# Key sums in head pairs without a pack, and the second matrix of the first expert rounded later, by ScalarE

## The chip, the cores and the metric

The kernel runs on one core of a Trainium2 chip. The time is that of one launch in microseconds on the device; three launches of the kernel before took 662.1, 662.74 and 663.9, the median is 662.74.

## What is computed

A random-feature attention of 8 batches, 8 heads, 576 positions and 64 values a head feeds a layer of 8 experts, of which each token uses one. From the reference, cut:

```python
q_p, k_p = (phi(q_s), phi(k_s))                # exp(proj - max), 128 features
kv = np.einsum('bhsm,bhsd->bhmd', k_p, v)
z = np.sum(k_p, axis=2)
num = np.einsum('bhsm,bhmd->bhsd', q_p, kv)
den = np.einsum('bhsm,bhm->bhs', q_p, z)[..., None] + 1e-06
x = (num / den)                                # 4608 tokens of 512
logits = xn @ en.T / tau                       # 8 experts
h = np.maximum(x[mask] @ w1[e], 0.0)           # 512 -> 1024
out[mask] = gate_w[mask, None] * (h @ w2[e])   # 1024 -> 512
```

## The kernel before

**Two stages.** To about 220 us a loop `for i in range(43)` does the attention, 128 tokens a tile, 36 tiles; the query side runs 6 iterations behind the key side (`LAG`). Iteration 31, say, makes the key features of tile 31, the query features of tile 25 and the results of tile 24. After the loop the experts run, 38 steps of 128 tokens, until the end of the span.

**One iteration.** TensorE projects keys and queries (`proj`), VectorE takes row maxima (`nmk`, `nmq`, L331), ScalarE takes exponentials (`ftk`, `ftq`, L338). The query features are turned by TensorE (`qtr`, L400, into the bank pair `nub`) and copied out half by ScalarE, half by VectorE (`qp`, L405). `num` (L417) multiplies them with the key sums `kvs` into `nub`; `num_out` on VectorE divides (`rr`, then `xr` L432 and `lg` L435). TensorE's next `qtr` writes the same banks, so it waits for `lg`.

**Key sums.** Two sequences of a batch pair are open at a time (b = 0, 1), and eight times in the loop one is closed: ScalarE copies the sums `kva` of even and odd heads to `kvs` (L361, two copies); GpSimd packs the values without their sum column into `xgp` (L363); in the next iteration TensorE turns the pack (`kvtr`, L372), VectorE copies it out (L376), TensorE multiplies with the expert vectors (L384), and VectorE writes these logits of the keys into `kvs` (L390). A head takes 73 columns of `kvs`: 64 values, their sum, 8 logits. The turns stand in iterations 6, 10, 15, 19, 24, 28, 33 and 37.

**Routing.** Every three iterations a group of three tiles is routed (`routed(g)`), a generator that is taken on in steps over the following iterations: GpSimd adds logits (L449) to `raw`; VectorE picks the expert (`mx`, `raw` L460, `sel` L465); TensorE counts; VectorE makes `base` (L481); GpSimd makes positions from it (L484, L449, L494) and scatters the rows of `xr`, one tile each, to memory (`xs`, L496). `xr` has 6 buffers: `xr` of tile 24, which VectorE writes in iteration 31, is written over tile 18's, whose scatter must have landed. VectorE and GpSimd (L425) wait for that.

**First expert.** From iteration 28 the eight weight parts of the expert that most of the tokens chose so far are loaded on SP (`first_weights(n)`, tile `rf`, 512 KB each; even n is the first matrix w1, odd n the second, w2), and in the iteration behind rounded to `h` (w1 by ScalarE L535, w2 by VectorE L537), with the remainder `l` by GpSimd in four pieces (L540). A matrix has two `rf` buffers. From iteration 37 on the generator `first_steps` fills TensorE with two steps of that expert; its w2 is multiplied only behind the loop. TensorE then needs a third tile of rows (`fs_x`), which SP loads when the last scatter has landed.

**Order.** The queues of all engines are filled in the order in which the code is called. Lists by iteration hold work that is put off: `mid`, `after`, `then`, `ends` run at four places of an iteration, and within a list in the order of the appends.

Of the kernel before, what the change touches and what calls it, by code (L numbers as in the profile page):

```python
# [55 lines left out]
def attention_moe(ctx: ExitStack, tc: tile.TileContext, qT, kT, v1, omT, emb, tau, w1q, w2q, xs, out):  # L56
# [222 lines left out]
    with ExitStack() as c1:  # L279
# [77 lines left out]

        def kv_closed(sb, b):
# [63 lines left out]
        def num_out(i):
# [6 lines left out]
            nc.vector.tensor_scalar(rr, pn[:, :, :, D], EPS, None, op0=ALU.add)  # L429
# [213 lines left out]
        later, fill = None, first_steps()  # L643
# [8 lines left out]
        for i in range(END + 1):  # L652
            iq = i - LAG
            st["now"] = i
            n = iq - 3 * GPICK - 7
            if 0 <= n < 2 * NQ:
                first_weights(n)
# [78 lines left out]
            if 0 <= n < 2 * NQ:  # L736
                at(ends, i + 1).append((first_split, n))
# [446 lines left out]
```

## Time and profile before

| | us |
|---|---|
| median of three launches | 662.74 |
| the profiled execution | 658.2 |
| its span, first to last instruction | 656.4 |
| TensorE busy | 631.7 (96%) |
| VectorE busy | 497.3 (76%) |
| ScalarE busy | 416.9 (64%) |
| GpSimd busy | 328.5 (50%) |

The granted clock of TensorE is 0.996 of its full level over the span. Busy time is a mean over two stages with different limits: within the loop ScalarE and VectorE are nearly always busy, behind it TensorE alone is. A row of the timeline gives the start, the duration, engine, line, operation, output<-input, count, and in brackets how long the engine sat idle before it and what released it.

### The profile page before, as it was taken

How to read it: one execution, taken by the hardware profiler on the slowest of the kernel's cores; microseconds unless marked ns; L12 is line 12 of the kernel's file. 1: busy time of each engine (PE TensorE's matmuls, PEld its weight loads, DVE VectorE, ACT ScalarE, POOL GpSimd, SP SyncE). 2: the span in 40 equal slices, each digit the busy share in tenths (PEclk: the TensorE clock that was granted, in tenths of full speed). 3: DMA queues.
4: the chain of work that ended last, by engine and by line, in shares of the span. 5: the costliest groups of instructions: out<-in, count | busy, mean ns of one | idle time of the engine just before them, and what ended most of it. 6: DMA issues, size and time to landing. Idle time of an engine off the chain costs nothing. (4 is left out here: it accounts for less than half of the span.)

```text
span 656.4 us, 18641 instructions
## 1 busy us (share of the span) xinstructions
PE 631.7 (96%) x6339; PEld 532.1 (81%) x6340; DVE 497.3 (76%) x952; ACT 416.9 (64%) x1074; POOL 328.5 (50%) x414
## 2 busy tenths in 40 slices
PE   8999999998889999999999999999999999999993
PEld 7899999988877787888788888888888888888872
DVE  4789888899888736778787777777768787777771
ACT  6899899899877236645656565656555656565430
POOL 2013443448885425474556364646455554646352
PEclk9999999999999999999999999999999999999998
DMA  7547667678832388588898888978697878887710
GB/s 252 177 148 228 196 202 212 214 243 285 261 125 97 118 308 259 156 237 198 237 211 223 208 227 190 240 193 232 178 244 184 236 192 196 225 208 212 187 64 34
DMA packets 142362, 131.89 MB, mean 201 GB/s; under 512 B 106742, under 2 KB 106870, under 8 KB 142272
## 3 DMA queue, kind: packets, MB, share of 16 engines
q1 hardware_dynamic: 135808, 110.04, 62.8%
q0 software_dynamic: 6320, 20.38, 7.9%
q8 instruction: 57, 0.93, 0.6%
q10 hardware_dynamic: 144, 0.26, 0.2%
q14 instruction: 33, 0.27, 0.1%
HBM read 83.78 MB, written 21.97 MB: 161 GB/s over the span
## 5 line engine op out<-in xcount | busy, mean ns | idle before, releaser
L241 PE MATMUL nu<-w2h,hl 128*128 (+1 forms) x288 | 113.9, 395 | 0.4 <-DVE hl L948 0.4
L241 PE MATMUL nu<-w2h,hh 128*128 (+1 forms) x288 | 113.9, 396 | 0.0
L241 PE MATMUL nu<-w2l,hh 128*128 (+1 forms) x288 | 113.8, 395 | 0.0
L241 PE MATMUL pa<-w1h,xl 128*128 (+1 forms) x280 | 110.8, 396 | 0.4 <-DVE xl L947 0.4
L241 PE MATMUL pa<-w1h,xh 128*128 (+1 forms) x280 | 111.1, 397 | 0.0
L241 PE MATMUL pa<-w1l,xh 128*128 (+1 forms) x280 | 110.6, 395 | 0.0
L909 ACT ACTIVATE pl<-pa 128x512 uint16<-128x512 uint16 x68 | 40.1, 594 | 94.2 <-PE pa L241 56.0
L905 DVE TENSOR_REDUCE wd<-t 128x1024 uint16<-128x1024 uint16 x68 | 90.0, 1325 | 1.7 <-DMA t<-pl 1.7
L338 ACT ACTIVATE ftk<-pjk,nmk 128x128 f32<-128x128 f32 x288 | 84.9, 427 | 6.3 <-DVE nmk L331 6.0
L207 POOL TENSOR_TENSOR w1l<-raww,w1h 128x1024 f32 x34 | 83.7, 2461 | 7.4 <-DVE w1h L206 5.5
L905 DVE TENSOR_REDUCE pl<-pa 128x512 uint16<-128x512 uint16 x68 | 46.6, 688 | 51.6 <-ACT pl L909 51.5
L338 ACT ACTIVATE ftq<-pjq,nmq 128x128 f32<-128x128 f32 x288 | 80.0, 430 | 8.7 <-DVE nmq L331 7.8
L207 POOL TENSOR_TENSOR w2l<-raww,w2h 128x1024 f32 x34 | 82.1, 2415 | 2.4 <-issue 2.4
L327 PE MATMUL pjq<-om,qt 64*128 64x128 f32 x576 | 75.6, 283 | 1.1 <-ACT ftk L338 0.7
L327 PE MATMUL pjk<-om,kt 64*128 64x128 f32 x576 | 76.3, 285 | 0.3 <-DVE om L602 0.3
L944 ACT ACTIVATE hh<-wd 128x1024 fp32r<-128x1024 f32 x34 | 36.1, 1062 | 60.2 <-DVE wd L905 54.3
L327 PEld LDWEIGHTS pjk<-om,kt 64*128 64x128 f32 x576 | 65.1, 190 | 2.9 <-DVE om L602 0.6
L271 POOL DMA_INDIRECT y<-xgp x20 | 22.7, 1136 | 87.6 <-DVE xgp L248 84.1
L241 PEld LDWEIGHTS nu<-w2h,hl 128*128 128x128 f32 x288 | 54.0, 188 | 13.9 <-DVE hl L948 0.8
L327 PEld LDWEIGHTS pjq<-om,qt 64*128 64x128 f32 x576 | 63.9, 188 | 1.6 <-ACT ftk L338 0.9
L241 PEld LDWEIGHTS nu<-w2l,hh 128*128 128x128 f32 x288 | 54.1, 188 | 13.1
L241 PEld LDWEIGHTS nu<-w2h,hh 128*128 128x128 f32 x288 | 54.1, 188 | 13.0
(311 smaller groups left out, 1270.0 us busy)
## 6 DMA issues: line engine op xcount, KB each, us to landing
raww<-w1q SPq DMA_DIRECT2D x38, 512.0 KB, 3.9
raww<-w2q SPq DMA_DIRECT2D x38, 512.0 KB, 5.2
qt<-qT SPq DMA_DIRECT2D x36, 256.0 KB, 4.3
kt<-kT SPq DMA_DIRECT2D x35, 256.0 KB, 3.0
xgp<-xs SPq DMA_DIRECT2D x20, 260.5 KB, 2.8
xg<-xs SPq DMA_DIRECT2D x18, 260.5 KB, 2.9
rf<-w1q SPq DMA_DIRECT2D x4, 512.0 KB, 5.6
rf<-w2q SPq DMA_DIRECT2D x4, 512.0 KB
```

Source lines behind the costliest of these rows:

```text
L207: il = nc.gpsimd.tensor_tensor(at(l, dp), raw, at(h, dp).bitcast(F32), op=ALU.subtract)
L241: done.append(nc.tensor.matmul(dst, x[:, c * P : (c + 1) * P], ws.rearrange("p o f -> p (o f)"), start=(begin and i == 0 and k == 0), stop ...
L271: w = nc.gpsimd.indirect_dma_start(out=out, out_offset=bass.IndirectOffsetOnAxis(ap=xg[:, PAY - 1 : PAY].bitcast(I32), axis=0), in_=xg[:, ...
L327: nc.tensor.matmul(st["pj" + w, i, a][:, c, :], st[w, i][r, c, :], om[r, :], start=True, stop=True)
L338: nc.scalar.activation(ft[:, h, :], pj[:, h, :], AF.Exp, bias=nm[:, h : h + 1])
L905: nc.vector.tensor_reduce(to, src.unsqueeze(2), axis=AX.X, op=ALU.max)
L909: nc.scalar.activation(planes[1][:, o : o + 512], halved(src)[:, :, 1], AF.Copy)
L944: nc.scalar.activation(hh, wd[:, 0:F], AF.Relu)
```

## The change

Even heads now keep their sum column ahead of the values, odd heads behind; `kvs` is laid out as four pairs of 146 columns: logits, sum, values of the even head, then values, sum, logits of the odd one. The 128 values of a pair touch, so TensorE turns them from `kvs` itself, and GpSimd's pack is gone. `num`, `num_out` and the logits' copy use views to match. All four roundings of w2 go from VectorE to ScalarE. Two tables say when a part is loaded (`WLOAD`, by iteration) and rounded (`WSPLIT`; 1 stands for the list `ends`, 0 for `mid`). Parts of w1 keep their iterations (ends of 29, 31, 33 and 35), those of w2 go from the ends of 30, 32, 34 and 36 to the middle of 37, 38, 40 and 41. The loads stand behind an iteration's other loads, where they stood ahead.

```diff
+WLOAD = {28: (0,), 30: (2, 1), 32: (4, 3), 34: (6,), 39: (5,), 40: (7,)}
+WSPLIT = {0: (1, 29), 2: (1, 31), 4: (1, 33), 6: (1, 35), 1: (0, 37), 3: (0, 38), 5: (0, 40), 7: (0, 41)}
...
         def kv_closed(sb, b):
-            kvs[sb, b] = p1.tile([P, H, D + 1 + E], F32, name=f"kvs{sb}_{b}", tag="kvs", bufs=2)
-            for a in range(2):
-                nc.scalar.activation(kvs[sb, b][:, 4 * a : 4 * a + 4, 0 : D + 1], kva[sb, b, a], AF.Copy)
-            kvc = xgp[NPRE][:, 0:DM].rearrange("p (h d) -> p h d", h=H)
-            nc.gpsimd.tensor_copy(
-                kvc.rearrange("p (c a) d -> p a c d", a=2), kvs[sb, b][:, :, 0:D].rearrange("p (a c) d -> p a c d", a=2)
-            )
+            kvs[sb, b] = p1.tile([P, 4, 2 * HW], F32, name=f"kvs{sb}_{b}", tag="kvs", bufs=2)
+            nc.scalar.activation(kvs[sb, b][:, :, E : HW], kva[sb, b, 0], AF.Copy)
+            nc.scalar.activation(kvs[sb, b][:, :, HW : HW + D + 1], kva[sb, b, 1], AF.Copy)
...
-                nc.tensor.transpose(tr[:, c * P : (c + 1) * P], kvc[:, 2 * c : 2 * c + 2, :].rearrange("p a d -> p (a d)"), ident)
+                nc.tensor.transpose(tr[:, c * P : (c + 1) * P], kvs[sb, b][:, c, E + 1 : E + 1 + P], ident)
...
         def first_split(n):
             q, (_, h, l) = n // 2, W[("w1", "w2")[n % 2]]
             raw = st["rf", n]
-            if n % 2 == 0:
-                nc.scalar.activation(h[:, 0, q, :], raw, AF.Copy)
-            else:
-                nc.vector.tensor_copy(h[:, 0, q, :], raw)
+            nc.scalar.activation(h[:, 0, q, :], raw, AF.Copy)
...
+        for n, (late, i) in WSPLIT.items():
+            at(ends if late else mid, i).append((first_split, n))
...
-            n = iq - 3 * GPICK - 7
-            if 0 <= n < 2 * NQ:
-                first_weights(n)
             if i < 2 or i >= 4:
                 load(i + (4 if i < 2 else 2))
             if i in (3, 4):
                 loadq(i - 3)
             loadq(iq + 2 if i > LAG - 1 else -1)
+            for n in WLOAD.get(i, ()):
+                first_weights(n)
...
-            if 0 <= n < 2 * NQ:
-                at(ends, i + 1).append((first_split, n))
```

The table `WSPLIT` is put into the lists before the loop; the old code appended a rounding at the end of an iteration, behind the routing steps that were listed already. So GpSimd's queue changes at the end of iteration 29 not only by the absence of the pack. Before (`xr_3047` is the row buffer of tile 18, `xr_3611` that of tile 22):

```order
L425 COPY xr_3611<-ids 128x1
L484 TENSOR_TENSOR base_3628<-base_3628,sel_127 128x24
L449 TENSOR_TENSOR base_3628<-base_3628 128x3x4
L449 TENSOR_TENSOR base_3628<-base_3628 128x3x2
L449 TENSOR_TENSOR pos_3632<-base_3628 128x3
L494 CAST posi_3636<-pos_3632 128x1
L496 DMA xs<-xr_3047,posi_3636 38016x576
L540 TENSOR_TENSOR w1l<-rf_3356,w1h 128x256 x4
L425 COPY xr_3744<-ids 128x1
```

And after, the same place on GpSimd (tile 18 is `xr_3042`, tile 22 `xr_3603`):

```order
L433 COPY xr_3603<-ids 128x1
L545 TENSOR_TENSOR w1l<-rf_3356,w1h 128x256 x4
L492 TENSOR_TENSOR base_3625<-base_3625,sel_127 128x24
L457 TENSOR_TENSOR base_3625<-base_3625 128x3x4
L457 TENSOR_TENSOR base_3625<-base_3625 128x3x2
L457 TENSOR_TENSOR pos_3629<-base_3625 128x3
L502 CAST posi_3633<-pos_3629 128x1
L504 DMA xs<-xr_3042,posi_3633 38016x576
L433 COPY xr_3738<-ids 128x1
```

The remainder of part 0, which waits for ScalarE's rounding, has moved ahead of the positions and the scatter of tile 18. Part 6 does the same at the end of iteration 35. On ScalarE in iteration 41 stood before, in a row (`ex` are the first steps' exponentials, `ftq` the query features):

```order
L553 ACTIVATE hp_4698<-fs_a_4826 128x512
L261 ACTIVATE ex_5169,totalp<-xgp_103,rt_p 128x8
L261 ACTIVATE ex_5171,totalp<-xgp_104,rt_p 128x8
L405 ACTIVATE qp_1_5029<-nub 128x512
L338 ACTIVATE ftq_0_5071<-pjq_0_5019,nmq_0_5036 128x128 x4
```

And after:

```order
L263 ACTIVATE ex_5161,totalp<-xgp_103,rt_p 128x8
L263 ACTIVATE ex_5163,totalp<-xgp_104,rt_p 128x8
L406 ACTIVATE qp_1_5016<-nub 128x512
L542 ACTIVATE w2h<-rf_4894 128x1024
L340 ACTIVATE ftq_0_5063<-pjq_0_5006,nmq_0_5028 128x128
```

A rounding has come between the copy of the turned queries and the features of the next ones; the same stands in iterations 37, 38 and 40. On GpSimd the remainders of w2 follow there. Before, between the scatters of tile 29 and tile 30 (`xr_4564` and `xr_4666`):

```order
L496 DMA xs<-xr_4564,posi_4982 38016x576
L462 COPY xr_4666<-raw_4899 128x8
L462 COPY xr_4770<-raw_4899 128x8
L462 COPY xr_4882<-raw_4899 128x8
L425 COPY xr_5064<-ids 128x1
L484 TENSOR_TENSOR base_5081<-base_5081,sel_127 128x24
```

And after (`xr_4538` and `xr_4639`):

```order
L504 DMA xs<-xr_4538,posi_4969 38016x576
L470 COPY xr_4639<-raw_4879 128x8
L470 COPY xr_4748<-raw_4879 128x8
L470 COPY xr_4862<-raw_4879 128x8
L545 TENSOR_TENSOR w2l<-rf_4894,w2h 128x256 x4
L433 COPY xr_5056<-ids 128x1
L492 TENSOR_TENSOR base_5073<-base_5073,sel_127 128x24
```

The remainder of part 7 stands there now. Those of parts 1, 3 and 5 stand between there and the scatters of iteration 36; before, that stretch held one, of part 7.

## Rows read from the trace of the kernel before

**Rows 1.** Windows: busy us (count) of PE, PEld, DVE, ACT, POOL; clock, DMA, GB/s.

```profile
160.00:170.00 10.00, 8.88 (x215) 8.27 (x214) 9.54 (x24) 9.74 (x34) 7.50 (x20) 1.00 0.87 280
200.00:210.00 10.00, 9.35 (x154) 7.79 (x150) 8.00 (x23) 6.88 (x26) 7.64 (x28) 1.00 0.22 82
220.00:230.00 10.00, 10.00 (x58) 8.19 (x58) 7.68 (x53) 2.72 (x5) 2.95 (x3) 1.00 0.40 138
```

**Rows 2.** Timelines of POOL, PEld and ACT around the turn of iteration 24.

```profile
115.89 0.62 POOL L363 COPY xgp<-kvs 128x512 f32<-128x512 f32 x1 [5.51 <-ACT kvs L361]
...
116.56 0.42 PEld L372 LDWEIGHTS kvtr<-ident,xgp 128*128 128x128 f32 x4 [0.27 <-POOL xgp L363]
...
122.35 0.60 ACT L405 ACTIVATE qp<-nub 128x512 f32<-128x512 f32 x1 [1.84 <-PE pjk L327]
```

**Rows 3.** Timeline of DVE in iterations 30 to 32.

```profile
154.25 0.69 DVE L331 TENSOR_REDUCE nmk<-pjk 128x4 f32<-128x512 f32 x1 [0.22 <-PE pjk L327]
...
157.82 0.69 DVE L432 TENSOR_TENSOR xr<-nub,rr 128x512 f32<-128x512 f32 x1
...
158.77 0.70 DVE L460 TENSOR_TENSOR raw<-raw,mx 128x24 f32<-128x24 f32 x1
...
161.09 0.68 DVE L405 COPY qp<-nub 128x512 f32<-128x512 f32 x1
```

**Rows 4.** Lines L537 and L465: count, ns min/median/max, first and last start.

```profile
L537 DVE CAST w2h<-rf x4: 686/788/1187, 152.8 to 188.3; 128x1024 fp32r<-128x1024 f32 x4
...
L465 DVE SCALAR_TENSOR_TENSOR sel<-raw,iotm x12: 173/183/645, 46.6 to 218.8; 128x24 bf16<-128x24 f32 x12
```

**Rows 5.** Timeline of PE, the turn of the queries in iteration 37.

```profile
188.52 0.71 PE L400 MATMUL nub<-ident,ftq 64*128 64x64 f32 x16 [0.60 <-DVE lg L435]
```

**Rows 6.** Timeline of ACT: roundings of w1, query features of iterations 40 and 41.

```profile
148.62 1.14 ACT L535 ACTIVATE w1h<-rf 128x1024 fp32r<-128x1024 f32 x1
...
184.06 1.14 ACT L535 ACTIVATE w1h<-rf 128x1024 fp32r<-128x1024 f32 x1
...
206.62 2.18 ACT L338 ACTIVATE ftq<-pjq,nmq 128x128 f32<-128x128 f32 x8 [1.13 <-DVE nmq L331]
...
211.22 2.18 ACT L338 ACTIVATE ftq<-pjq,nmq 128x128 f32<-128x128 f32 x8 [0.89 <-DVE nmq L331]
```

**Rows 7.** Timeline of POOL from iteration 29 to the last scatters.

```profile
150.23 1.05 POOL L496 DMA_INDIRECT xs<-xr,posi  x1 [0.86 <-POOL posi L494]
151.31 3.31 POOL L540 TENSOR_TENSOR w1l<-rf,w1h 128x256 fp32r<-128x256 f32 x4
...
183.48 0.23 POOL L484 TENSOR_TENSOR base<-base,sel 128x24 f32<-128x24 f32 x1
...
185.37 1.05 POOL L496 DMA_INDIRECT xs<-xr,posi  x1 [0.56 <-POOL posi L494]
...
193.00 2.78 POOL L540 TENSOR_TENSOR w2l<-rf,w2h 128x256 fp32r<-128x256 f32 x4
...
198.80 0.23 POOL L484 TENSOR_TENSOR base<-base,sel 128x24 f32<-128x24 f32 x1 [0.93 <-DVE base L481]
...
213.30 0.23 POOL L484 TENSOR_TENSOR base<-base,sel 128x24 f32<-128x24 f32 x1 [3.16 <-DVE base L481]
...
222.94 0.98 POOL L496 DMA_INDIRECT xs<-xr,posi  x1 [3.23 <-DVE runi L761]
```

**Rows 8.** Line L496 in 140:162, then in 190:222; and the page's DMA issues.

```profile
DMA to landing us min/median/max: 5.5/5.8/6.5
...
DMA to landing us min/median/max: 2.7/2.8/4.9
...
rf<-w1q SPq DMA_DIRECT2D x4, 512.0 KB, 5.6
```

**Rows 9.** Timelines of POOL and PE where the third tile of rows arrives.

```profile
231.57 0.60 POOL L765 DMA_DIRECT2D xs<-w1l  x1 [5.08 <-DMA xgp<-xs]
...
232.02 0.60 PE L227 MATMUL fs_x<-ident,xgp 128*128 128x128 f32 x4
```

More of the change, by code (lines that the diff above doesn't have):

```diff
@@ L356, in kvmm, with spread @@
                     )
+        HW = D + 1 + E
+        def spread(x, *dims):
+            return bass.AP(tensor=x.tensor, offset=x.offset, ap=[x.ap[0], *([a, n] for a, n in dims)])
         def kv_closed(sb, b):
-            kvs[sb, b] = p1.tile([P, H, D + 1 + E], F32, name=f"kvs{sb}_{b}", tag="kvs", bufs=2)
-            for a in range(2):
-                nc.scalar.activation(kvs[sb, b][:, 4 * a : 4 * a + 4, 0 : D + 1], kva[sb, b, a], AF.Copy)
-            kvc = xgp[NPRE][:, 0:DM].rearrange("p (h d) -> p h d", h=H)
-            nc.gpsimd.tensor_copy(
-                kvc.rearrange("p (c a) d -> p a c d", a=2), kvs[sb, b][:, :, 0:D].rearrange("p (a c) d -> p a c d", a=2)
-            )
-            st["kvc", sb, b] = kvc
+            kvs[sb, b] = p1.tile([P, 4, 2 * HW], F32, name=f"kvs{sb}_{b}", tag="kvs", bufs=2)
+            nc.scalar.activation(kvs[sb, b][:, :, E : HW], kva[sb, b, 0], AF.Copy)
+            nc.scalar.activation(kvs[sb, b][:, :, HW : HW + D + 1], kva[sb, b, 1], AF.Copy)
         def kv_turn(sb, b):
-            kvc = st["kvc", sb, b]
             st["kvtr", sb, b] = tr = ps.tile([P, 512], F32, name=f"kvtr{sb}_{b}", tag="kv0")
             for c in range(4):
-                nc.tensor.transpose(tr[:, c * P : (c + 1) * P], kvc[:, 2 * c : 2 * c + 2, :].rearrange("p a d -> p (a d)"), ident)
+                nc.tensor.transpose(tr[:, c * P : (c + 1) * P], kvs[sb, b][:, c, E + 1 : E + 1 + P], ident)
         def kv_turned(sb, b):
@@ L390, in kv_logits_out @@
             nc.vector.tensor_copy(
-                kvs[sb, b][:, :, D + 1 :].rearrange("p (a c) e -> p c a e", a=2),
+                spread(kvs[sb, b].rearrange("p c w -> p (c w)"), (2 * HW, 4), (HW + D + 1, 2), (1, E)),
                 st["kve", sb, b].rearrange("p c (a e) -> p c a e", a=2),
@@ L407, in qcopy, with heads @@
                 tc.declare_no_dep(c.ins, st["cp", 1].ins.name, reason="another bank")
-        pn = nub[:, :, 0 : 4 * (D + 1 + E)].rearrange("p a (h w) -> p a h w", h=4)
+        flat = nub.rearrange("p a x -> p (a x)")
+        o0 = P + E // 2
+        pn = [nub[:, a, o : o + 4 * HW].rearrange("p (h w) -> p h w", h=4) for a, o in ((0, o0), (1, 0))]
+        def heads(o, at1, n):
+            x = 512 + at1 - o0 - o
+            return flat[:, o0 + o : o0 + o + 2 * x].rearrange("p (a x) -> p a x", a=2)[:, :, 0 : 4 * HW].rearrange("p a (h w) -> p a h w", h=4)[:, :, :, 0:n]
         def num(i):
@@ L417, in num @@
                         nc.tensor.matmul(
-                            pn[z * 64 : z * 64 + 64, a, h, :], st["qp", i, z][:, 4 * a + h, :], kvs[sb, int(b)][:, 4 * a + h, :],
+                            pn[a][z * 64 : z * 64 + 64, h, :], st["qp", i, z][:, 4 * a + h, :], kvs[sb, int(b)][:, h, a * HW : (a + 1) * HW],
                             start=True, stop=True,
@@ L428, in num_out @@
             rr = small.tile([P, 2, 4], F32, name=f"rr{i}", tag="rr", bufs=3)
-            nc.vector.tensor_scalar(rr, pn[:, :, :, D], EPS, None, op0=ALU.add)
+            nc.vector.tensor_scalar(rr.unsqueeze(3), heads(E, D, 1), EPS, None, op0=ALU.add)
             nc.vector.reciprocal(rr, rr)
@@ L432, in num_out @@
             nc.vector.tensor_tensor(
-                xr[:, 0:DM].rearrange("p (h a d) -> p a h d", a=2, d=D), pn[:, :, :, 0:D], by(D), op=ALU.mult,
+                xr[:, 0:DM].rearrange("p (h a d) -> p a h d", a=2, d=D), heads(E + 1, 0, D), by(D), op=ALU.mult,
             )
             nc.vector.tensor_tensor(
-                st["lg", g][:, gi].rearrange("p (a h) e -> p a h e", a=2), pn[:, :, :, D + 1 :], by(E), op=ALU.mult,
+                st["lg", g][:, gi].rearrange("p (a h) e -> p a h e", a=2), heads(0, D + 1, E), by(E), op=ALU.mult,
             )
@@ L642, in attention_moe @@
             at(ends, i).append((f,))
-        later, fill = None, first_steps()
+        for n, (late, i) in WSPLIT.items():
+            at(ends if late else mid, i).append((first_split, n))
+        fill = first_steps()
         def go(d, *key):
@@ L1152, in layout @@
         rows = slice(0, D) if u == 4 else slice(D, P) if u == 5 else slice(0, P)
-        v1[:, u, rows, :, :D] = v[:, u - (u > 4), rows]
-        v1[:, u, rows, :, D] = 1
+        v1[:, u, rows, 0::2, 1:] = v[:, u - (u > 4), rows, 0::2]
+        v1[:, u, rows, 0::2, 0] = 1
+        v1[:, u, rows, 1::2, :D] = v[:, u - (u > 4), rows, 1::2]
+        v1[:, u, rows, 1::2, D] = 1
     v1 = v1.reshape(NSB * (TPS + 1), P, H, D + 1)
```

## The prediction

> **What bounds the kernel now.** I read the windows first. From 160 to 170 us VectorE and ScalarE are busy for 9.54 and 9.74 of 10 us and TensorE has gaps (8.88); from 200 to 210 TensorE is nearly full (9.35) while the others are not; behind 220 it has no gap at all [rows 1]. So a microsecond saved on VectorE or ScalarE counts up to iteration 36, when the key side ends, and from iteration 39 on the end moves only as TensorE's queue moves. TensorE's queue has one fixed appointment behind the loop: it turns the third tile of rows at 232.02, and those rows were in at 231.57, 0.45 us before [rows 9]. They are loaded when the last scatter has landed, so GpSimd's queue sets the other edge of the same instant. I therefore follow two clocks to 232: the loop's, and GpSimd's. Behind that the work is the same before and after.
>
> All sums are in the profiled execution: 658.2 us, of which the span is 656.4. Its 658.2 is 4.5 below the median of the launches, 662.74; I add the difference that I find to the median.
>
> **The pack.** GpSimd packs for 0.62 us, and TensorE's turn stood 0.27 us for it [rows 2]; the same wait stands at the other turns. Taking the copy away lets the turn start when the projections end, since the pack ended 0.27 us behind them; ScalarE's copies were done before the pack began. It counts only where TensorE is late: in iteration 24 ScalarE then sat 1.84 us for TensorE [rows 2], and iterations 6, 15 and 33 have the same pattern (double key sums). In the other four VectorE runs through and nothing is gained. That is 4 x 0.27 = 1.1 us: 0.8 before iteration 29 and 0.3 in iteration 33. The bounds are 0 (ScalarE's second copy takes the pack's place) and the whole pack, 4 x 0.62 = 2.5; I take the wait itself. The new strides of `kvs` and `nub` keep the counts and sizes of every copy and product, and the sums still come from the same banks; I cost them at nothing.
>
> **VectorE's four roundings.** They last 0.69 to 1.19, together about 3.4 us [rows 4]. What each was worth is what stood behind it. In iteration 30, VectorE waited 0.22 for TensorE right after it [rows 3]; the gain there is hidden anyway by the next item. In iteration 32 ScalarE has no gap [rows 1]; I take 0.1 of 0.69. In iteration 36 the next copy needs the turned queries, whose turn started at 188.52 on the release of `lg`, not of the rounding [rows 5]: 0. In iteration 34 VectorE is the bound and 0.6 of 0.69 counts (neighbouring rows overlap by 0.1). With them goes a second cost: `raw` took 0.70 in iteration 31 while GpSimd worked on remainders [rows 3, 7], and `sel`, whose median is 0.183, 0.645 [rows 4]. The same pair stands in iteration 34. Free of the remainders they are some 0.9 shorter together. In iteration 34 that goes, since the remainder of part 4 is then done early: 0.6 + 0.9 = 1.5 us. In iteration 31 it stays, because part 2's remainder moves right beside it.
>
> **What the order adds in iteration 29.** The remainder of part 0 now stands ahead of `base` on GpSimd. It waits for ScalarE's rounding, which ends at 148.62 + 1.14 = 149.76 [rows 6]; it takes 2.78 rather than the 3.31 that it took beside VectorE's rounding [rows 7]; from the start of `base` to the scatter pass 185.37 - 183.48 = 1.89 us [rows 7]. So tile 18's scatter starts at 149.8 + 2.8 + 1.9 = 154.5, where it was 150.23. Scatters of this stretch land 5.5 to 6.5 us after their start [rows 8]: at 160.0 to 161.0, say 160.5. VectorE writes `xr` of tile 24 over that buffer, which it did at 157.82 [rows 3]. Before, the landing came by 156.7; now VectorE stands, and behind it the logits, the next turn of the queries, their copies: iteration 32 starts 2.7 us later than before. [...]
>
> From there: +2.7, -0.1 (iteration 32), -0.3 (the turn in 33), -1.5 (34) = **+0.8 us in iteration 35**, still without the 0.8 saved before iteration 29.
>
> **ScalarE in the tail.** Its four new roundings (about 1.1 each, the form of L535) fall between the copy of the queries and the next features, where ScalarE waited 1.13 and 0.89 us for VectorE's maxima [rows 6]; two earlier gaps are as wide. I cost them at nothing. Uncovered they would cost 4.5 us. Behind them on ScalarE are only the features, and TensorE waits for those. Part 5 is loaded an iteration before its rounding, 206.62 - 211.22 apart, 4.6 us; such a load took 5.6 to land [rows 6, 8], so ScalarE may stand up to 1 us there. The DMA share is 0.22 then [rows 1]; I take 0.
>
> **GpSimd in the tail.** Between `base` at 183.48 and the last three scatters at 222.94 lie 39.5 us, of which GpSimd waited 0.93 + 3.16 + 3.23 = 7.3 [rows 7]; 32.1 us is work. The new queue begins this chain with part 6's remainder, which waits for ScalarE at 184.06 + 1.14 + 0.8 = 186.0 [rows 6]. Its work is 32.1 - 0.6 (pack) - 0.5 (part 6 beside no VectorE rounding) + 3 x 2.78 (parts 3, 5, 7; part 1 is in part 7's old place) [rows 7] = 39.3 us, and the waits are gone, because the chain is always behind. The last scatters start at 186.0 + 39.3 = 225.3, 2.4 later. The third tile is in at 231.57 + 2.4 = 234.0, and TensorE, due at 232.02 and late by less than that, turns it 1.9 later than before.
>
> **Sum.** +1.9 in the tail, -0.8 from the first three turns: **+1.1 us**. The profile would be 659.3, the launch 662.74 + 1.1 = 663.8 us.
>
> **Rivals.**
>
> *The scatter lands in time.* If it lands in 2.8 to 4 us as in the quiet stretch [rows 8], `xr` is not held beyond 157.8, and iteration 35 comes at -1.9 rather than +0.8: TensorE's appointment at -0.8, with the first turns -1.6: 661.1. If the pair in iteration 31 shrinks too, 1.4 more: 659.7. For it: part 1's load no longer stands in iteration 29. Against: all five scatters from 140 to 161 took 5.5 or more. GpSimd's queue caps this gain, the loop itself would have 3 us. Chance 0.25.
>
> *The burst of loads (slower).* Parts 2 and 1 are now issued back to back at the end of iteration 30's loads, about 153.5 to 155, by their place on SP just ahead of tile 18's scatter; before, 512 KB at most stood beside one. A second 512 KB at 250 to 300 GB/s [rows 1] is some 2 us more: landing after 8.5, iteration 32 at +5.2, the appointment at +4.4, in all +3.6: 666.3. It decides from a landing of 6.9 us: there the sum passes 0.3%. For it: the DMA share is already 0.87 [rows 1]. Chance 0.25. [...]
>
> *The pack is not saved, or part 5 comes late.* ScalarE's second copy holds TensorE as long as the pack did (+0.8), or ScalarE stands for part 5: 664.6. Chance 0.1.
>
> **How the numbers follow.** Forecast 0.40 with its own range of 662.3 to 665.3 (the landing 5.5 to 6.5, half a microsecond in GpSimd's chain), rivals 0.25, 0.25, 0.1. The predicted time is the forecast's, 663.8. The range reaches from the middle of the first rival to that of the second: 660.3 to 666.3. 0.3% is 2.0 us, about what a measurement of this kernel can tell from no change. Faster by more needs a time below 660.7: the lower part of the first rival, 0.16. Slower by more needs more than 664.7: nearly all of the burst and the upper end of the others, 0.30. Within: 0.54.
>
> **What would show it.** Right: in the profile after, VectorE's `xr` of iteration 31 or GpSimd's `ids` copy stands 2 to 3 us for the landing of tile 18's scatter, which starts near 154; iteration 34 is about 1.5 us shorter; GpSimd's waits of 3.16 and 3.23 near the loop's end are gone and the last three scatters start 1 to 2 us later; TensorE waits a little at `fs_x`. The turns wait for nothing on GpSimd. Wrong: `xr` in iteration 31 doesn't wait; ScalarE's w2 roundings push the query features; GpSimd is idle again before the last scatters, and then the loop's clock decides.

## The result, and the profile after

The changed kernel takes 670.66 us (median of five launches, 668.51 to 671.94), the kernel before 662.94 in the same comparison: a ratio of 1.0111 with a 95% interval of 1.0087 to 1.0135. Two later comparisons gave 1.008 [1.0051, 1.0109] and 1.0083 [1.0066, 1.010]. The change makes the kernel slower by 0.8 to 1.1%, some 5.4 to 7.7 us; 663.8 with a range of 660.3 to 666.3 was forecast.

One thing must be known before traces are compared. The chips fall into two kinds for this kernel. On some, the kernel before takes 657 to 658 us, on others 663 to 665 (each chip was met in one batch of runs only, so the chip and the occasion can't be told apart); its profiled execution of 658.2, on which the prediction rests, is like the launches of the first kind, and the changed kernel's first trace comes from the second. Both kernels are longer there in iterations 13 to 28, so this difference has no part in the result (shown below, by a trace of the kernel before from a chip of the second kind). Ratios below are always to the kernel before on the same chip, and the ledger of the time is made from two traces of one chip.

Windows of the changed kernel, with the columns of [rows 1]: the first row answers to 160 to 170 us there, and the others are finer.

```profile
160.00:170.00 10.00, 4.53 (x102) 4.27 (x100) 3.81 (x10) 4.66 (x15) 4.44 (x11) 0.85 0.71 236
...
160.00:162.00 2.00, 2.00 (x66) 1.93 (x62) 1.56 (x4) 2.00 (x10) 1.47 (x6) 1.00 0.93 164
162.00:164.00 2.00, 1.06 (x16) 0.86 (x16) 0.00 (x0) 1.40 (x6) 0.56 (x1) 1.00 0.94 358
164.00:166.00 2.00, 0.00 (x0) 0.00 (x0) 0.00 (x0) 0.94 (x1) 0.00 (x0) 1.00 1.03 403
166.00:168.00 2.00, 0.00 (x0) 0.00 (x0) 0.35 (x1) 0.00 (x0) 0.41 (x2) 0.75 0.62 241
168.00:170.00 2.00, 1.47 (x22) 1.47 (x24) 1.90 (x6) 0.31 (x1) 2.00 (x4) 0.50 0.04 17
170.00:172.00 2.00, 1.56 (x16) 1.30 (x16) 1.97 (x5) 1.10 (x5) 1.72 (x4) 0.50 0.00 0
172.00:174.00 2.00, 2.00 (x41) 2.00 (x42) 1.54 (x3) 1.89 (x9) 0.49 (x4) 0.54 0.42 117
174.00:176.00 2.00, 2.00 (x58) 1.93 (x54) 1.44 (x6) 2.00 (x9) 0.23 (x1) 1.00 0.40 156
```

In [rows 1] VectorE and ScalarE were busy for 9.54 and 9.74 of these 10 us. Now VectorE stands from 161.7 to 167.65, GpSimd from 162.6 to 167.6, TensorE from 163.1 to 168.5, and ScalarE from 164.9 to 169.7, while the DMA share is 0.93 to 1.03 up to 166. TensorE's granted clock is 0.51 from 167 to 168, 0.50 up to 172 and 0.54 in the two us behind. What they stand for is in the timelines. GpSimd (answers to [rows 7]), VectorE ([rows 3]), TensorE ([rows 5]) and SP's queue, iteration 31 of the changed kernel:

```profile
154.12 2.80 POOL L545 TENSOR_TENSOR w1l<-rf,w1h 128x256 fp32r<-128x256 f32 x4 [6.17 <-ACT w1h L542]
...
158.77 1.05 POOL L504 DMA_INDIRECT xs<-xr,posi  x1 [0.56 <-POOL posi L502]
...
167.59 0.18 POOL L433 COPY xr<-ids 128x1 int32<-128x1 int32 x1 [5.03 <-DMA xs<-xr,posi]
...
158.48 0.68 DVE L406 COPY qp<-nub 128x512 f32<-128x512 f32 x1
...
161.50 0.20 DVE L438 RECIPROCAL rr<-rr 128x8 f32<-128x8 f32 x1
167.65 0.69 DVE L440 TENSOR_TENSOR xr<-nub,rr 128x512 f32<-128x512 f32 x1 [5.95 <-DMA xs<-xr,posi]
...
171.08 0.67 DVE L406 COPY qp<-nub 128x512 f32<-128x512 f32 x1
...
168.53 1.12 PE L401 MATMUL nub<-ident,ftq 64*128 64x64 f32 x16 [5.47 <-DVE lg L443]
...
157.80 0.34 SPq L537 DMA_DIRECT2D rf<-w1q  x1
158.41 0.34 SPq L537 DMA_DIRECT2D rf<-w2q  x1
```

The remainder of part 0 (L545) ends just ahead of the routing step, tile 18's scatter starts at 158.77, 8.8 us later VectorE may write `xr`, and the iteration takes 12.60 us from copy to copy of the queries, where it took 6.15 (from 154.94 to the copy at 161.09 [rows 3]). Parts 2 and 1 of the weights were asked for one behind the other right ahead of the scatter.

### The profile page after: what moved, and what is told of

Its sections match the earlier page's. It is cut to its first block, busy times and chain, and to the rows that moved or that the text cites. A ratio compares the mean times of both kernels' runs of the same rounds, so it can differ in the third digit from the quotient of the medians.

```text
span 669.0 us, 18617 instructions
## 1 busy us (share of the span) xinstructions
PE 633.8 (95%) x6339; PEld 536.4 (80%) x6340; DVE 494.5 (74%) x948; ACT 421.4 (63%) x1078; POOL 321.3 (48%) x406
## 5 line engine op out<-in xcount | busy, mean ns | idle before, releaser
L329 PE MATMUL pjk<-om,kt 64*128 64x128 f32 x576 | 78.8, 294 | 0.8 <-DVE om L607 0.5
L329 PEld LDWEIGHTS pjk<-om,kt 64*128 64x128 f32 x576 | 67.0, 197 | 3.4 <-DVE om L607 0.8
```

The lines of the kernel that those rows point to most:

```text
L329: nc.tensor.matmul(st["pj" + w, i, a][:, c, :], st[w, i][r, c, :], om[r, :], start=True, stop=True)
```

## Where the time goes, on one chip

The length of an iteration is the time from its copy `qp` on VectorE to the next one. From the traces e13 (kernel before) and e14 (changed), both of one chip, whose launches differ by 5.6 us (665.12 and 670.74):

| stretch | forecast | e14 less e13 |
|---|---|---|
| iterations 7 to 28 | -0.8 | -1.7 |
| 29 and 30 | 0 | -0.4 |
| 31 | +2.7 | +6.4 |
| 32 to 36 | -1.9 | -0.2 |
| 37 to 41 | not the bound | +2.6 |
| sum to iteration 42 | | +6.7 |

The two spans differ by 6.8 us. By the loop's own clock the forecast's stretches add up to 0.0, the measured ones to 6.7: iteration 31 is 3.7 of the difference, iterations 37 to 41 are 2.6, iterations 32 to 36 1.7, and the early ones take 1.3 off. The forecast took GpSimd's chain for the later clock at `fs_x`, came to +1.9 there and so to +1.1 in all.

## The experiments

All verdicts are ratios to the kernel before in the same comparison. The lengths of the iterations that differ, in us (chips of the first kind above, of the second below):

| kernel | 31 | 32 | 34 | 37 | 38 | 40 | 41 |
|---|---|---|---|---|---|---|---|
| e10, before | 6.09 | 5.24 | 6.51 | 5.69 | 5.54 | 4.41 | 5.00 |
| e1, layout alone | 6.10 | 5.22 | 5.87 | 5.36 | 5.48 | 4.41 | 4.99 |
| e9, layout, ScalarE rounds in place | 6.33 | 5.41 | 5.28 | 5.66 | 5.50 | 4.41 | 4.99 |
| e2, weights alone | 11.99 | 5.87 | 5.19 | 6.98 | 5.67 | 7.72 | 6.47 |
| e3, w1 behind the routing | 5.45 | 7.11 | 5.24 | 5.36 | 5.53 | 7.15 | 6.34 |
| e4, loads spread | 9.18 | 6.96 | 5.27 | 7.13 | 5.48 | 7.30 | 5.24 |
| e11, parts 5 and 7 late | 6.52 | 5.12 | 5.17 | 5.36 | 5.49 | 6.34 | 6.24 |
| e12, the same, asked early | 6.53 | 5.11 | 5.17 | 5.36 | 5.48 | 4.69 | 5.24 |
| e13, before | 6.54 | 5.05 | 6.44 | 6.40 | 5.48 | 5.04 | 4.76 |
| e14, changed | 12.93 | 5.51 | 6.11 | 6.46 | 5.67 | 6.02 | 5.76 |
| e5, changed | 11.48 | 6.66 | 6.22 | 6.67 | 6.13 | 6.61 | 5.24 |
| e6, no late remainders | 5.79 | 7.03 | 5.22 | 6.01 | 8.46 | 6.43 | 5.14 |
| e7, w1 behind, loads spread | 5.69 | 6.32 | 5.22 | 6.00 | 8.47 | 5.86 | 5.24 |
| e8, w2 in 34 to 38 | 5.80 | 5.53 | 6.21 | 5.36 | 6.83 | 4.77 | 5.52 |
| e15, as e12 | 6.56 | 5.11 | 5.22 | 5.55 | 5.49 | 4.71 | 5.82 |

**The two halves.** e1 takes the change's `kvs`, `num` and `num_out` and leaves the weights as they were; e2 the reverse, with the pack. From the changed kernel to e1 (the roundings of w2 go back to VectorE besides):

```diff
-        for n, (late, i) in WSPLIT.items():
-            at(ends if late else mid, i).append((first_split, n))
...
-            for n in WLOAD.get(i, ()):
-                first_weights(n)
...
+            n = iq - 3 * GPICK - 7
+            if 0 <= n < 2 * NQ:
+                first_weights(n)
...
+            if 0 <= n < 2 * NQ:
+                at(ends, i + 1).append((first_split, n))
```

> Only the layout of the key sums is changed; loads, roundings and remainders of the first expert stand as before the change. Where the changed kernel went wrong, its trace shows three places: iterations 13 to 28 end 4.3 us later than in the trace before, iteration 31 takes 12.6 us instead of 6.2, and iterations 37 to 42 lose another 3.5. Theory W (all that counts comes from the weights, and the early 4.3 us are what one execution differs from another): the time is 662.1, that is 0.8 below the kernel before by my step on the pack, within 1 us of it either way; iterations 31 and 32 and 37 to 42 look as before. Theory L (the new layout itself makes the turns and the iterations behind them longer): 666 to 667, and iterations 13, 15, 19, 22, 24 and 28 show the lengths of the changed kernel (5.74, 7.55, 6.80, 6.44, 7.49, 6.50 us).

> Only the loads, roundings and remainders of the first expert are changed; the key sums keep the layout and the pack of before. Theory W: 670 to 672 (the changed kernel's time, or 0.8 above it), with the scatter that iteration 31 needs landing 8 to 9 us after its start. Theory L: 666 to 667, since the early 4 us stay away, and iteration 31 still takes 12 to 13 us.

The layout alone: 656.07 against 657.61, 0.9975 [0.9958, 0.9992], a gain of 1.5 us. The weights alone: 666.87, 1.0145 [1.010, 1.0189], a loss of 9.3. So the whole loss is the weights', and the layout is a small gain. Iterations 13, 15, 19, 22, 24 and 28 of e1 and e2 have the lengths of the kernel before within 0.2 us, but for iteration 13 of e2 (5.71 where e10 has 5.18).

**Order or loads.** e3 puts the first matrix's splits back behind the routing steps; e4 leaves the order and asks for parts 1 and 3 an iteration earlier.

In e3 the second piece stands at the end of the loop's body; the last two lines are e4.

```diff
-            at(ends if late else mid, i).append((first_split, n))
+            if not late:
+                at(mid, i).append((first_split, n))
...
+            for n, (late, j) in WSPLIT.items():
+                if late and j == i + 1:
+                    at(ends, j).append((first_split, n))
...
-WLOAD = {28: (0,), 30: (2, 1), 32: (4, 3), 34: (6,), 39: (5,), 40: (7,)}
+WLOAD = {28: (0,), 29: (1,), 30: (2,), 31: (3,), 32: (4,), 34: (6,), 39: (5,), 40: (7,)}
```

> The changed kernel, but the first matrix's splits (parts 0, 2, 4, 6) stand behind the routing steps of their iteration on GpSimd, as before the change; loads and everything else as changed. Theory O (the remainder ahead of the routing steps starts tile 18's scatter 4.3 us late, and that is most of it): the scatter starts about 4.3 us earlier against its iteration, lands in time or within 1.2 us of it even if it takes 8.8 us, iteration 31 takes 6.2 to 7.4 us instead of 12.6, and the time falls by 5 to 6.5 to 664 to 666. Theory B (the loads of parts 2 and 1 asked for together hold up whatever scatter runs beside them): iteration 31 or the next still waits 3 us or more, and the time falls by less than 3.

> The changed kernel, but parts 1 and 3 are asked for one iteration earlier than parts 2 and 4 (29, 30, 31, 32 instead of both at 30 and both at 32), so that no two 512 KB loads are asked for together; the order on GpSimd as changed. Theory B: tile 18's scatter lands some 6 us after its start instead of 8.8, iteration 31 takes 9 to 10 us, and the time falls by 2.5 to 4 to 667 to 668. Theory O: the scatter still starts late and what is gained is below 1.5; 669 to 671.

e3: 659.31, 1.003 [1.0003, 1.0057]. e4: 663.82, 1.0092 [1.0055, 1.0129]. Against the sum of the two halves, 665.4, an estimate for the changed kernel on this chip, e3 is 6.1 us faster and e4 1.6: the gain that theory O had for e3, and less than theory B had for e4. Iteration 31 takes 5.45 us with the old order and the burst, 9.18 with the new order and no burst, 11.99 with both (e2, which keeps the pack). GpSimd's scatter of tile 18 and VectorE's `xr` of tile 24 in e4, then the same two in e3, then in e2:

```profile
154.61 1.05 POOL L504 DMA_INDIRECT xs<-xr,posi  x1 [0.56 <-POOL posi L502]
...
160.00 0.69 DVE L440 TENSOR_TENSOR xr<-nub,rr 128x512 f32<-128x512 f32 x1 [2.53 <-DMA xs<-xr,posi]
```

```profile
149.55 1.05 POOL L504 DMA_INDIRECT xs<-xr,posi  x1 [0.56 <-POOL posi L502]
...
156.98 0.69 DVE L440 TENSOR_TENSOR xr<-nub,rr 128x512 f32<-128x512 f32 x1
```

```profile
154.95 1.05 POOL L498 DMA_INDIRECT xs<-xr,posi  x1 [0.56 <-POOL posi L496]
...
163.26 0.69 DVE L434 TENSOR_TENSOR xr<-nub,rr 128x512 f32<-128x512 f32 x1 [5.49 <-DMA xs<-xr,posi]
```

Without the burst VectorE stands 2.53 us for the landing; with it 5.49 in e2 and 4.85 (e5), 5.95 (the first trace) and 6.26 (e14) in the changed kernel; with the old order it doesn't stand at all, burst (e3) or not (e7). The order opens the wait, the burst doubles it.

The order costs e4 more than this wait: iteration 32 takes 6.96 us there and 5.22 in e1. TensorE had stood too, for 1.90 us up to 160.9, and its granted clock, 1.00 up to 162, was 0.52 to 0.50 up to 168. Windows of e4:

```profile
162.00:164.00 2.00, 0.84 (x10) 0.55 (x8) 1.93 (x5) 0.60 (x3) 1.72 (x4) 0.52 0.87 277
...
166.00:168.00 2.00, 2.00 (x45) 2.00 (x43) 1.10 (x4) 2.00 (x10) 0.00 (x0) 0.50 0.12 44
```

Iteration 32 of e3 takes 7.11 us at a granted clock of 1.00 (windows from 150 to 170); TensorE stands 1.26 us in it before it projects the queries. In e7 the same stop, 0.87 us, is put down to the load of the query tile, in e3 to an older release; that the weights hold up that load is likely but not shown.

Iteration 37 has the order's price once more, at part 6: 6.98 us in e2 and 7.13 in e4, 5.36 in e3. In e4 VectorE's `xr` stands 1.60 us for a scatter, in e2 TensorE's turn of the key sums stands 1.59 us for the pack, which waits behind the remainder on GpSimd. VectorE in e4:

```profile
196.93 0.69 DVE L440 TENSOR_TENSOR xr<-nub,rr 128x512 f32<-128x512 f32 x1 [1.60 <-DMA xs<-xr,posi]
```

**The changed kernel on the chip of e6 to e8**, without an edit.

> The changed kernel itself, on the chip of the other runs, whose kernel before took 657.6 where that of the first comparison took 662.9. If the two halves of the change add up (the layout alone was 1.5 below the kernel before, the weights alone 9.3 above), 665.4, that is a ratio near 1.012; if they hinder or help each other by more than 2 us it is below 663.4 or above 667.4. Its iterations 13 to 29 should then be as long as those of the kernel before (theory W), and not 4 us longer as in the first trace (theory L, which the layout alone has already contradicted).

668.71 against 663.34, 1.008 [1.0051, 1.0109]. This batch came to a chip of the second kind, so the absolute figures of the expectation don't apply. Taken as differences, the halves add up to 7.8 us and 5.4 were measured, 2.4 less; the first comparison had 7.7, so the halves may as well add up. The early iterations were the long ones again, which theory W, as I had worded it there, did not expect; e13 settles it.

**What lengthens iterations 40 and 41.** e6 is e3 without GpSimd's remainders of parts 5 and 7.

```diff
+        nc.gpsimd.memset(w2l[:, 0, 2:4, :].bitcast(F32), 0.0)
...
-            for c in range(0, F, 256):
+            for c in range(0, 0 if n in (5, 7) else F, 256):
```

> The kernel with the first matrix's splits behind the routing steps (659.3 on this chip), without GpSimd's remainders of parts 5 and 7 of the second matrix in iterations 40 and 41, which are left at zero; ScalarE still rounds both parts there. Theory P (VectorE's small routing and norm steps stand while GpSimd's remainder runs beside them, ScalarE's exponents stand behind those norms, and TensorE behind ScalarE's copy of the queries): the subtraction of raw falls from 1.91 to 0.2 us, iterations 40 and 41 fall from 7.15 and 6.34 to about 5.4 and 5.0 us, and the time falls by 3 to 656. Theory S (ScalarE's rounding of 1.05 us in front of its features is what lengthens them): the two iterations stay within 0.7 us of 7.15 and 6.34, and the time falls by less than 1.

666.06, 1.0045 [1.003, 1.0061]; e3 had 1.003. The time didn't fall, so by that the expectation failed; the rows say more. VectorE, GpSimd and ScalarE in iteration 40 of e3, and then VectorE and ScalarE of e6:

```profile
207.55 0.17 DVE L467 TENSOR_REDUCE mx<-raw 128x3 f32<-128x24 f32 x1
207.75 1.91 DVE L468 TENSOR_TENSOR raw<-raw,mx 128x24 f32<-128x24 f32 x1
209.59 0.69 DVE L257 TENSOR_SCALAR rt_p<-rt_p 128x2 f32<-128x2 f32 x1
...
207.45 2.80 POOL L545 TENSOR_TENSOR w2l<-rf,w2h 128x256 fp32r<-128x256 f32 x4
...
204.71 1.06 ACT L542 ACTIVATE w2h<-rf 128x1024 fp32r<-128x1024 f32 x1 [0.88 <-DMA rf<-w2q]
...
210.51 0.30 ACT L263 ACTIVATE ex<-xgp,rt_p 128x8 f32<-128x8 f32 x1 [2.19 <-DVE rt_p L258]
```

```profile
214.94 0.24 DVE L468 TENSOR_TENSOR raw<-raw,mx 128x24 f32<-128x24 f32 x1
215.11 0.16 DVE L257 TENSOR_SCALAR rt_p<-rt_p 128x2 f32<-128x2 f32 x1
...
214.26 1.06 ACT L542 ACTIVATE w2h<-rf 128x1024 fp32r<-128x1024 f32 x1 [2.35 <-issue]
```

`raw` falls from 1.91 to 0.24 us with GpSimd's remainder gone, `rt_p` from 0.69 to 0.16, and the exponents no longer wait. The two runs come from different kinds of chip; e7, from e6's chip and with the remainders, has 0.68 and 0.75, and its exponents wait 0.59. Theory P is right about the steps. But in e6 ScalarE stands 2.35 us in front of its rounding of part 5, asked for at 208.37 on SP (the profile names no releaser; in e11 the same wait is put down to the load), and iteration 38 took 8.46. There the remainder of part 3 meets `sel`; VectorE and GpSimd in iteration 38 of e7:

```profile
198.62 3.16 DVE L475 TENSOR_TENSOR sel<-iotm,mx 128x24 bf16<-128x24 f32 x1
...
198.98 2.76 POOL L545 TENSOR_TENSOR w2l<-rf,w2h 128x256 fp32r<-128x256 f32 x4
```

The same step, 0.18 us in iteration 31 of e3, ends at 201.78 here, when GpSimd's four pieces are done (201.74). Which step is hit changes from run to run: in iteration 38 in e6 and e7, in 40 in e2 to e5; in the first trace of the changed kernel and in e14 no such step takes over 0.8 us.

Iterations 40 and 41 of e14, which the ledger rests on, show a third wait. VectorE and ScalarE there:

```profile
220.74 0.69 DVE L440 TENSOR_TENSOR xr<-nub,rr 128x512 f32<-128x512 f32 x1 [1.21 <-DMA xs<-xr,posi]
221.68 0.49 DVE L468 TENSOR_TENSOR raw<-raw,mx 128x24 f32<-128x24 f32 x1
222.10 0.74 DVE L257 TENSOR_SCALAR rt_p<-rt_p 128x2 f32<-128x2 f32 x1
...
218.65 1.06 ACT L542 ACTIVATE w2h<-rf 128x1024 fp32r<-128x1024 f32 x1 [1.12 <-DMA rf<-w2q]
```

`xr` of iteration 40 stands for a scatter as that of iteration 31 did: 1.21 us here, 1.27 in e2, 0.97 in e3, 0.93 in e4, 0.17 in e11, none in e5 to e7 and e12. No run isolates this wait.

**Both mended, and a better place for w2.** e7 is e3 with e4's table. e8 is e3 with the second matrix in iterations 34, 36, 37 and 38.

```diff
+WLOAD = {28: (0,), 30: (2,), 31: (1,), 32: (4,), 33: (3,), 34: (6,), 35: (5,), 37: (7,)}
+WSPLIT = {0: (1, 29), 2: (1, 31), 4: (1, 33), 6: (1, 35), 1: (0, 34), 3: (0, 36), 5: (0, 37), 7: (0, 38)}
```

> The kernel with the first matrix's splits behind the routing steps (659.3), and besides parts 1 and 3 asked for one iteration earlier than 2 and 4. Theory B2 (with the order mended, what the two loads asked for together still cost is TensorE's wait for the queries of iteration 33, 1.3 us of waiting in a 7.1 us iteration that has 5.2 in the kernel with the layout alone): that iteration takes 5.2 to 5.6 us, the time is 657 to 658. If the loads are not it, 659 to 660 and 7 us again.

> The change's layout, the first matrix's splits behind the routing steps, and the second matrix's four parts rounded by ScalarE and split by GpSimd in iterations 34, 36, 37 and 38, asked for one at a time at 31, 33, 35 and 37, so that no load stands with another, and none of its remainders runs in iterations 40 and 41. From the kernel with the layout alone (656.1): 0.65 less at iteration 31 and 0.65 at 34, where VectorE's casts stood beside GpSimd's remainders; 654.5 to 655.5 if nothing else turns up, a ratio of 0.995 to 0.997. A rival: ScalarE's rounding in iteration 34 or 36, in front of its features, costs as much as it saves: 656 to 658.

e7: 665.20, 1.0027 [1.0011, 1.0043]; iteration 32 is 6.32 where e6 on the same chip has 7.03, so of the 1.9 us expected from the loads 0.7 came. e8: 662.22, 0.9981 [0.9965, 0.9998], a gain, but the smaller one that the rival had: iteration 34 takes 6.21 where e15, on a chip of the same kind, has 5.22.

**Who rounds, and the late parts by themselves.** e9 is the layout with one line changed, ScalarE for VectorE. e11 is the layout with only parts 5 and 7 as in the change; e12 asks for these two in iterations 36 and 37.

The first piece is e9, the rest e11; e12 differs from e11 in `WLOAD`, which is `{36: (5,), 37: (7,)}`.

```diff
-            if n % 2 == 0:
-                nc.scalar.activation(h[:, 0, q, :], raw, AF.Copy)
-            else:
-                nc.vector.tensor_copy(h[:, 0, q, :], raw)
+            nc.scalar.activation(h[:, 0, q, :], raw, AF.Copy)
...
+LATE = {5: 40, 7: 41}
+WLOAD = {39: (5,), 40: (7,)}
...
+            if n % 2 == 0 or n >= 5:
...
+        for m, j in LATE.items():
+            at(mid, j).append((first_split, m))
...
+            if 0 <= n < 2 * NQ and n not in LATE:
+                first_weights(n)
...
+            for m in WLOAD.get(i, ()):
+                first_weights(m)
```

> The kernel with the layout alone, and ScalarE instead of VectorE rounding the second matrix's parts, at the times and places where VectorE did it before the change. So the change's third part without its moves. If who rounds is what counts (theory R, my step on VectorE's four roundings: 0.6 of cast in iteration 34, and 0.1 or nothing in the other three), iteration 34 falls from 5.87 us in the kernel with the layout alone to 5.2 to 5.4, the rest stays, and the ratio to the kernel before is 0.996 to 0.997 where the layout alone had 0.9975. If ScalarE's 1.05 us come out of its own path (it was busy 9.7 of 10 us from 160 to 170), iterations 31 to 33 grow by 0.3 to 1 each and the ratio is 0.998 to 1.000.

> The kernel with the layout alone, and only parts 5 and 7 of the second matrix late, as in the change: asked for in iterations 39 and 40, rounded by ScalarE and split by GpSimd in 40 and 41. Theory P+D (ScalarE stands for part 5's landing in front of its features, 0.9 to 2.4 us, and VectorE's subtraction of raw stands while GpSimd's remainder runs, up to 2.7 us, with ScalarE's exponents behind it): iteration 40 takes 6.4 to 7.7 us instead of 4.4, iteration 41 5.2 to 6.4 instead of 5.0, iteration 34 5.2 instead of 5.9; 1.5 to 3 us slower than the layout alone, a ratio of 1.000 to 1.002. Theory S (ScalarE's rounding of 1.05 us alone): iterations 40 and 41 grow by at most 0.5 each, and the ratio stays at 0.997 to 0.998.

> The same, but parts 5 and 7 are asked for in iterations 36 and 37, so that they have landed long before ScalarE rounds them in 40 and 41. Theory D (the landing is the larger part): iteration 40 falls to 4.6 to 5.2, the ratio is 0.997 to 0.999. Theory P (GpSimd's remainder beside VectorE's steps is the larger part): iteration 40 stays 1.5 us or more above 4.4, and the subtraction of raw or a step next to it takes 0.7 us or more there.

e9: 655.87 against 657.93, 0.997 [0.9957, 0.9983], not told apart from e1. Iteration 34 fell to 5.28 and the ratio is 0.997, as theory R had it; 31 to 33, 36 and 37 grew by 0.1 to 0.4 each, somewhat less than the rival had. e11: 0.9977 [0.9962, 0.9991], e12: 0.9962 [0.9945, 0.9979]. ScalarE in iteration 40 of e11, then of e12:

```profile
205.59 1.06 ACT L543 ACTIVATE w2h<-rf 128x1024 fp32r<-128x1024 f32 x1 [2.25 <-DMA rf<-w2q]
```

```profile
203.19 1.05 ACT L543 ACTIVATE w2h<-rf 128x1024 fp32r<-128x1024 f32 x1
```

Asked for early, part 5 costs no wait, and iteration 40 takes 4.69 us instead of 6.34, 41 takes 5.24 instead of 6.24: theory D. ScalarE's rounding and GpSimd's remainder together are worth 0.3 us in iteration 40 there (4.41 before), so on the rounding itself the forecast had been right. The launches show less of it. e11 has the long iterations of theory P+D, but the ratio of theory S, that of the layout alone, and the median of e12 is 1.1 us below that of e11 where these two iterations give 2.65. From `fs_x` to the end the traces differ by up to 2.3 us without a pattern (422.1 to 424.4 in all 17), so what an iteration gives can be lost from view there.

**The chips.** Without edits: the kernel before on two more chips, and beside it on the second the changed kernel and e12.

> The kernel before, for its trace on the chip of this batch. Two chips showed 657.6 and 663.3 for it, and every kernel whose trace comes from the second had iterations 13, 15, 19, 22, 24 and 28 at 5.8, 7.5, 6.8, 6.4, 7.5 and 6.4 us, where those of the first had 5.2, 6.8, 6.4, 5.2, 6.8 to 7.0 and 6.2, whatever the layout. If the early 4.3 us between my two traces are the chip's (theory W), this trace has the long ones when its time is near 663, and the short ones when it is near 657. If they are the layout's (theory L), the short ones on either chip.

> The kernel before, once more for its trace. So far its traces come from chips on which it takes 657 to 658 us, and the changed kernel's from chips on which the kernel before takes 663. If this chip is of the second kind, theory W expects iterations 13, 15, 19, 22 and 24 at about 5.8, 7.5, 6.8, 6.4 and 7.5 us in the kernel before too, and iteration 29 begun some 3.5 us later than in the earlier traces of it (144.2 and 144.3); theory L expects 5.2, 6.8, 6.4, 5.2 and 6.9 as in those. If it is of the first kind, the short ones, and the next run decides.

> The changed kernel beside it. On a chip of the first kind theory W expects the short iterations 13 to 28, iteration 29 begun within 0.5 us of the kernel before, and all that is lost behind it: 10 to 11 us by the end of the loop, 1 to 2 of which come back behind it, a ratio of 1.012 to 1.014 (the weights alone had 1.0145, the layout alone 0.9975). Theory L expects it some 3.5 us late at iteration 29 there as well. On a chip of the second kind: iteration 29 as late as in the kernel before, a ratio of 1.008 to 1.012.

> The best of the variants (the layout, first matrix as before the change, parts 5 and 7 of the second matrix rounded by ScalarE in iterations 40 and 41 and asked for in 36 and 37), for the same chip: a ratio of 0.995 to 0.998 whichever kind the chip is of, if what it gains is not of one kind of chip; 0.999 or more if the gain belongs to the first kind alone.

e10 took 658.12 and has the short iterations (5.18, 6.82, 6.40, 5.18 and 6.88 for 13, 15, 19, 22 and 24); e13 took 663.97 and has 6.57, 7.26, 7.22, 6.43 and 7.24. It begins iteration 29 at 150.32, the changed kernel beside it at 149.20. So the early 4.3 us go with the chip and not with the layout, and theory L is out. e14: 1.0083 [1.0066, 1.010]. e15: 661.56 against 665.12, 0.9948 [0.9935, 0.9961]. This version has the lowest ratios, 0.4 to 0.5% faster than the kernel before on both kinds of chip; on the first its interval overlaps those of e1 and e9, so that it beats the layout alone isn't shown.

## Why the prediction was wrong, step by step

Two steps failed: the landing of tile 18's scatter, taken at 5.5 to 6.5 us and measured at 8.8, and the tail, where ScalarE's roundings with their loads were put at nothing and iterations 37 to 41 took 2.6 us more. Besides, GpSimd's chain was taken for the later clock and the loop was it. The direction was right, the size was not.

**The order in iteration 29: right, with the landing too small.** The scatter was to start 4.3 us late and VectorE's `xr` to stand 2.7 us for it. Without the burst it stood 2.53 (e4), the forecast's own case to 0.2. In the changed kernel it stood 4.85 to 6.26, with a landing of 7.7 to 9.2 (from the scatter's start to GpSimd's `ids` copy that waits for it). That is the second rival, which had a landing of 8.5 us and +5.2; the iteration is 6.4 longer. I gave it 0.25, an estimate, because no row of before showed two parts in flight beside a scatter; the rows did show the DMA share at 0.87 with one [rows 1], and a share of 1.03 with two is what followed. The same scatter landed after 5.3 us in e4 and after 8.2 in e2 with a second load beside it, and in e2 the DMA share is 0.99 and 1.04 from 159 to 163 and 0.22 in the two us behind.

**ScalarE and the second matrix in the tail: the other step that failed.** "I cost them at nothing" held for the roundings (0.3 us in iteration 40 of e12) and not for what comes with them: part 5 is asked for one iteration ahead and ScalarE stands for it 0.88 (e3) to 2.25 us (e11), 1.12 in e14, where I had named 1 at most and taken 0, and GpSimd's remainders stand beside VectorE's small steps. I had counted that contention only where the change takes it away (0.9 us in iteration 34) and not where it puts it. In e2 iterations 40 and 41 lose 3.3 and 1.5 us (the 1.3 of iteration 37 are the order's, at part 6); on the chip of the ledger 40 and 41 lose 1.0 each and 37 to 39 0.6 together. Of these terms only part 5's landing is isolated, by e11 and e12; how the rest divides between the remainders beside VectorE and the late scatter of iteration 40 stays open.

**GpSimd's chain as the bound: wrong.** It was to be always behind, with the waits of [rows 7] gone, and the end to move by it. GpSimd and TensorE at the loop's end of the changed kernel's first trace, then TensorE in e13 and e14:

```profile
237.49 0.98 POOL L504 DMA_INDIRECT xs<-xr,posi  x1 [1.94 <-DVE runi L765]
...
246.57 0.60 PE L229 MATMUL fs_x<-ident,xgp 128*128 128x128 f32 x4
```

```profile
239.38 0.60 PE L227 MATMUL fs_x<-ident,xgp 128*128 128x128 f32 x4
```

```profile
246.43 0.60 PE L229 MATMUL fs_x<-ident,xgp 128*128 128x128 f32 x4
```

GpSimd still waits for VectorE ahead of its last scatters, 1.94 instead of 3.23, so the loop sets the end, and `fs_x` comes 7.05 us later from e13 to e14, about as late as the loop is. In all 17 traces it comes 17.7 to 18.0 us behind the copy `qp` of iteration 42, with and without the late remainders.

**VectorE's roundings: right, but not in the changed kernel itself.** Iteration 34 falls from 6.51 to 5.19 (e2), 1.3 of the 1.5 forecast, through the cast of 0.69, a `raw` of 0.40 and a `sel` of 0.65 that become 0.18 each. VectorE in e10, then in e2:

```profile
177.35 0.40 DVE L460 TENSOR_TENSOR raw<-raw,mx 128x24 f32<-128x24 f32 x1
177.79 0.65 DVE L465 SCALAR_TENSOR_TENSOR sel<-raw,iotm 128x24 bf16<-128x24 f32 x1
...
178.79 0.69 DVE L537 CAST w2h<-rf 128x1024 fp32r<-128x1024 f32 x1
```

```profile
183.20 0.18 DVE L462 TENSOR_TENSOR raw<-raw,mx 128x24 f32<-128x24 f32 x1
183.41 0.18 DVE L467 SCALAR_TENSOR_TENSOR sel<-raw,iotm 128x24 bf16<-128x24 f32 x1
```

The two parts come apart: the layout alone already frees the pair of steps (5.87 in e1), and ScalarE for VectorE gives the other 0.6 (5.28 in e9). In the changed kernel itself iteration 34 takes 6.11 (e14, 0.3 less than e13), 6.22 (e5) and 7.06 (first trace). That isn't the chip's doing, since e6, e7 and e15 have 5.22 on such chips. In e14 VectorE stands 0.49 us for TensorE's `num`; what makes TensorE late there stays open.

**The pack: nearly the right size, by luck.** The layout is worth 1.5 us in launches against 1.1 forecast, but not through the turns. On chips of the first kind those up to iteration 28 gave 0.15 us each at most, iteration 33, where 0.3 was forecast, takes 6.80 us in e10 and 6.81 in e1, and iteration 29 began no earlier (117.1 us behind iteration 7 in e1, 117.0 in e10). GpSimd's queue is shorter by the pack of 0.62 [rows 2], and its work meets VectorE's at other places. VectorE's cast in iteration 30 of e10, and then of e1:

```profile
153.33 1.49 DVE L537 CAST w2h<-rf 128x1024 fp32r<-128x1024 f32 x1
```

```profile
153.16 0.90 DVE L543 CAST w2h<-rf 128x1024 fp32r<-128x1024 f32 x1
```

Iterations 29, 30, 34 and 37, shorter by 0.3 to 0.6 each than in e10, make the gain (iteration 29 takes 4.89 us in the first trace of before too, so its share is the least sure). That the shifted meeting of the two engines is the cause is read from such rows; no run isolates it. On the chip of the ledger 1.7 us came before iteration 29; why the layout counts there and not on the others stays open.

**The chance.** Slower by over 0.3% had 0.30, nearly all from the burst. The two halves of the loss, burst and tail, were each named and each taken for less likely than their absence; for both together the prediction had no case.

## To carry to other kernels

When work is moved on a queue, ask of each later transfer whether its landing is awaited by a buffer's next writer, and price the landing with everything that the new order puts in flight at once. Where GpSimd is given more work, list VectorE's small steps beside it: a step of 0.2 us took as long as four queued pieces of GpSimd's work (3.16 us in e7). Asking for the two late pieces three iterations earlier cost nothing here and took ScalarE's wait of 2.25 us away (e11 and e12).

## What the runs showed of the hardware that I had not expected

VectorE's small steps lasted over several GpSimd instructions in a row, not over one: 1.91 (e3), 2.75 (e5) and 3.16 us (e7) beside four pieces of 0.69 each, where they take 0.18 to 0.25 alone (2.75 is `raw`). The first ended 0.1 us behind the third piece, the other two 0.05 behind the fourth; in other executions the same step took 0.6 to 0.8 (0.70 in [rows 3]). `rt_p`, which has one input, is longer too: 0.69 in e3 and 0.16 in e6. The reduction `mx`, right ahead of the `raw` of 1.91 and beside the first piece, took 0.17.

The stop of 5.5 us on TensorE was followed by about 7 us at a granted clock of 0.50 to 0.54 (167 to 174), in which the turn of the queries took 1.12 us instead of 0.71 [rows 5]. Iteration 32, in which it ended, is 0.5 us longer on the chip of the ledger; in e4 TensorE stood 1.90 us up to 160.9, and its clock was 0.52 from 162 to 164 and 0.50 up to 168.

The same kernel differs by 5 to 7 us between chips, and its traces by 6.0 us before iteration 29 (e10 and e13), for a reason that stays open; on such a scale two traces must come from one chip.
